# Four transposing DMAs at another place in the tail, and another order of all operations, in a recurrent attention layer with a gated feed-forward

## The chip, the cores and the metric

The kernel runs on one core of one Trainium2 chip. The metric is the device time of one execution in microseconds. Three timed runs of the kernel before gave 998.56, 998.62 and 999.2 us; their median, 998.62 us, is its time.

## The reference

The input is one sequence of 2048 tokens with 640 features, in bf16. It goes through an attention layer with a recurrent memory and then through a gated feed-forward layer, each on the normalised input and each with the residual added.

```python
for s in range(n_seg):                      # 64 segments of 32 tokens
    h = concatenate([mem, xs])              # 8 memory rows, then the 32 tokens
    q, k, v = h @ Wq, h @ Wk, h @ Wv        # 32 heads of 128
    p = softmax(where(mask, q k^T * scale, -1e9))
    o = (p v) @ Wo                          # 40 rows of 640
    mem = o[:8]                             # goes into the next segment
    outs.append(o[8:])
h  = x + attention(layernorm(x))
gate, up = layernorm(h) @ W_gate, layernorm(h) @ W_up    # 640 -> 1728
h2 = h + (gate * (gate > 0) * up) @ W_down
```

The first 8 rows of a segment's output are the memory of the next one, so the 64 segments run one after another. Everything else (the projections of the tokens that are not memory, the feed-forward of finished tokens) can be done at other times.

## The kernel before, in words

**Stages.** The kernel first loads Wq, Wk, Wv and Wo (rows "Wq<-in_A_Wq_dram" and so on) and meanwhile projects part of the tokens ahead (`rest`, for the first nine of sixteen groups of 128 tokens). Then it runs the 64 segments (`segment`). In a segment, TensorE projects Q, K and V (line 1577, five steps for each of six banks, four matmuls of 128x512 per step on strips of 32 columns of the array), forms scores (1954, 1958), sums (1968), the product with V (1993, 1998), and the output projection (2027, 2046, 2063). ScalarE and VectorE evacuate PSUM between them (lines 1411 and 1412 are the two halves of one helper, `copy`), VectorE transposes Q and K (2076). Into the gaps of that chain the kernel puts work that is not urgent: `rest` for later tokens, the output rows of finished token groups (`rest_o`, 1661), and gate and up projections of finished token quarters (`ahead`, 1742), whose results wait in HBM (`scr_g`).

**The tail.** After the last segment the space of the attention weights is free. SyncE loads the feed-forward weights there: W_gate and W_up in three pieces each, in the order columns 512 to 895, 896 to 1663, 0 to 511 (`FPIECES`, loaded by `load_f`, issue line 2164), then W_down and the last 64 columns, and the results that were computed ahead (2177, 2180, 1767). TensorE computes what is left of the gates of the third quarter of tokens (`gates(2)`, matmuls at 1778), the down projections of three quarters (`downs`, 1834), then the gates and down projections of the last quarter (`gates(3)`, `downs(3)`). The last quarter's normalised rows lie in HBM (`scr_n`), and four transposing DMAs, one for each 128 tokens, bring them into `xn2T` with features on partitions (issue line 1771, operation name "xnld"); each can be issued once its rows are written. Line 1834 is the down projection with `again` (1555) as its second half, 1824 that of the last 128 tokens.

**What sets the order.** Nothing in the code is emitted in program order. Every operation is registered with its engine (or a choice of engines), its inputs and outputs, an assumed duration and a name. A list scheduler in the kernel (`_Sched.schedule`) then takes, for each engine in turn, the ready operation of the highest level; the order on each engine's queue, the bank or buffer that an operation gets, and the engine where there is a choice come out of it. An operation's level is the length of the longest chain of assumed durations behind it, plus a bias from a table, and a second bias for the name in one segment:

```python
o.level += self.bias.get(o.name, 0.0) + self.bias.get(f"{o.name}@{o.seg}", 0.0)
```

Segment numbers run from 1 to 64; 0 and below stand for the start, 65 for the tail. `BIAS` holds 3645 such numbers. The weight loads of the tail have biases of their own, 2000 less 20 for each load, set in `load_f`. Evacuations of PSUM are registered through `either`, and `ENGINE`, a table by name and by name and segment, says whether ScalarE ("act") or VectorE ("dve") has them; a name that is not in it goes to whichever the scheduler finds done first. SyncE issues nearly all DMAs, in the order of its queue, one after another.

Of the kernel before, what the change touches and what calls it, by code (L numbers as in the profile page):

```python
# [27 lines left out]
BIAS = {"sel2": -428.53, "ezero": 827.13, "ldxs0": 772.6, "ldxs1": -1075.19, "ldxa": 977.15, "ldxl": -444.97,  # L28
    "ldxx": 94.56, "ldxn": 296.11, "ldxx0": -425.81, "ldxst": -946.28, "ldxxm": -329.88, "ldmev": -440.02,
# [18 lines left out]
    "gx": -75.13, "gxrelu": -736.07, "gxev": -228.23, "gxst": -268.67, "ln2nd": -1166.07, "xnld": 1080.06,  # L48
    "gld": -294.56, "gu": 52.5, "relu": 1032.72, "gmul": -789.51, "roz": -16.73, "tn2go": 142.03,
# [1214 lines left out]
def build_kernel(nc, A_x, A_mem0, A_Wq, A_Wk, A_Wv, A_Wo, A_seg_len, B_x, B_W_gate, B_W_up,  # L1264
# [46 lines left out]
    sel2 = ar.alloc("sel2", [128, 64], BF16)  # L1311
# [21 lines left out]
    oTr = [ar.alloc(f"oTr{i}", [128, H, 32], BF16) for i in range(2)]  # L1333
# [63 lines left out]
    sc = _Sched()  # L1397
# [483 lines left out]
    for nm, b in (("ldxr", 9000.0), ("ldxr1", 8950.0)):  # L1881
        for t in ("", "s0", "s1", "a", "l", "x", "n", "T", "e"):
            sc.bias[nm + t] = b
# [369 lines left out]
```

## Time and profile before

| | us |
|---|---|
| median of the three timed runs | 998.62 |
| the profiled execution, as a whole | 995.62 |
| its span, first to last instruction | 993.9 |
| TensorE busy in it | 973.8 |
| VectorE busy | 618.3 |
| ScalarE busy | 502.4 |
| GpSimd busy | 112.5 |

The profiled execution took 1.72 us more than its span. A row of the timeline is one instruction, or several of one kind that follow each other ("x20"): start, length in us, engine, line, operation, output tile and input tiles, shape, and in brackets the idle time of the engine before it and what ended it. "SPq" is SyncE's queue, where a row is the issue of a DMA and not its transfer. "PEld" is the weight load of TensorE, which runs beside the matmuls; a matmul of 128x512 is recorded with some 379 ns though the next one may start 216 ns after it, so that TensorE can be called busy while it waits a little.

### The profile page before, as it was taken

What the parts mean: (1) busy time and instruction counts of PE and PEld (TensorE: products, weight loads), DVE (VectorE), ACT (ScalarE), POOL (GpSimd) and SP (SyncE); (2) the same over time, 40 slices, a digit from 0 to 9 for tenths busy, and PEclk for the clock granted to TensorE, in tenths of its full rate; (3) what the DMA queues carried; (4) which work ended last, traced back from release to release, by engine and by line L of the source; (5) the groups of instructions that cost most, each with busy time, mean ns of one, the idle gap of its engine ahead of it and who ended that gap; (6) DMA issues with size and microseconds to landing.
All of it is one profiled execution on the core that took longest, in us unless ns stands there. A gap on an engine that the chain in (4) does not pass through costs nothing.

```text
span 993.9 us, 54620 instructions
## 1 busy us (share of the span) xinstructions
PE 973.8 (98%) x25518; PEld 535.7 (54%) x24540; DVE 618.3 (62%) x1345; ACT 502.4 (51%) x1226; POOL 112.5 (11%) x264
## 2 busy tenths in 40 slices
PE   7989999999999999999999999999999999999998
PEld 4334565555555555655555556555555565543343
DVE  5835767768676766576666676767656766523232
ACT  2236555556565565555555565555555656521020
POOL 2341011111011011001000010000100000100000
PEclk9999999999999999999999999999999999999999
DMA  8996122223131323232232234333223352289211
GB/s 320 403 350 145 45 57 57 66 53 92 36 89 39 85 76 83 55 81 66 67 84 62 78 105 86 86 93 79 52 72 89 76 102 76 68 260 288 72 41 40
DMA packets 181553, 103.62 MB, mean 104 GB/s; under 512 B 126212, under 2 KB 177484, under 8 KB 181324
## 3 DMA queue, kind: packets, MB, share of 16 engines
q1 hardware_dynamic: 175948, 95.51, 34.5%
q10 hardware_dynamic: 5376, 4.63, 1.4%
q8 instruction: 196, 3.21, 1.3%
q14 instruction: 33, 0.27, 0.1%
HBM read 67.30 MB, written 29.75 MB: 98 GB/s over the span
## 4 chain that ended last, share of the span: by engine, by line
PE 90%; DMA 4%; SPq 3%; DVE 1%; issue 1%; ACT 0%; POOL 0%; ACTq 0%; DVEq 0%; POOLq 0%
PE ps L1577 49%; PE ps L2046 7%; PE ps L1742 7%; PE ps L2027 7%; PE ps L1834 4%; PE ps L1661 3%; PE ps L1778 3%; PE ps L1993 3%; DMA scr_qk<-stg 3%; PE ps L1555 2%; PE ps L1968 2%; PE ps L1954 1%; SPq L2164 1%; DMA Wq<-in_A_Wq_dram 1%; DMA scr_o<-osr 1%
## 5 line engine op out<-in xcount | busy, mean ns | idle before, releaser
L1411 ACT ACTIVATE tok<-ps 128x512 bf16<-128x512 f32 x216 | 128.2, 597 | 146.5 <-PE ps L1577 141.4
L1577 PE MATMUL ps<-Wk,xT 128*32 128x512 bf16 x2560 | 180.4, 379 | 0.4 <-ACT tok L1411 0.4
L1577 PE MATMUL ps<-Wv,xT 128*32 128x512 bf16 x2560 | 176.3, 379 | 0.0
L1577 PE MATMUL ps<-Wq,xT 128*32 128x512 bf16 x2560 | 170.1, 379 | 0.5 <-DVE tok L1412 0.3
L2076 DVE STREAM_TRANSPOSE QT<-tok 128x512 bf16<-128x512 bf16 x128 | 90.6, 708 | 47.5 <-ACT tok L1411 45.4
L1577 PEld LDWEIGHTS ps<-Wq,xT 128*32 128x32 bf16 x2560 | 70.6, 97 | 66.5 <-DVE xT L1691 9.1
L2076 DVE STREAM_TRANSPOSE KT<-tok 128x512 bf16<-128x512 bf16 x128 | 90.8, 709 | 24.6 <-ACT tok L1411 22.7
L1577 PEld LDWEIGHTS ps<-Wk,xT 128*32 128x32 bf16 x2560 | 68.4, 96 | 55.6 <-DVE xT L1691 2.9
L1963 ACT ACTIVATE E<-ps 128x224 bf16<-128x224 f32 x128 | 45.7, 357 | 81.4 <-PE ps L1958 77.7
L2046 PE MATMUL ps<-Wo,oT 128*32 128x160 bf16 x4096 | 83.5, 233 | 1.0 <-issue 1.0
L2046 PEld LDWEIGHTS ps<-Wo,oT 128*32 128x32 bf16 x4096 | 74.1, 97 | 15.5 <-ACT oT L1411 5.6
L2027 PE MATMUL ps<-Wo,oT 128*32 128x320 bf16 x2048 | 81.5, 300 | 0.9 <-DVE oT L1412 0.8
L1577 PEld LDWEIGHTS ps<-Wv,xT 128*32 128x32 bf16 x2560 | 61.0, 96 | 38.8 <-ACT tok L1411 0.7
L1412 DVE CAST oT<-ps 128x320 bf16<-128x320 f32 x124 | 55.0, 485 | 42.9 <-PE ps L1998 36.9
L1940 POOL COPY QT<-RS 128x256 bf16<-128x256 bf16 x64 | 25.7, 402 | 470.4 <-PE ps L1958 470.2
L1411 ACT ACTIVATE Vm<-ps 128x512 bf16<-128x512 f32 x122 | 72.0, 591 | 11.4 <-PE ps L1577 6.3
L1412 DVE CAST tok<-ps 128x512 bf16<-128x512 f32 x104 | 68.7, 661 | 9.6 <-PE ps L1577 9.3
L2027 PEld LDWEIGHTS ps<-Wo,oT 128*32 128x32 bf16 x2048 | 52.7, 96 | 27.3 <-DVE oT L1412 7.7
L1688 DVE CAST_PREDICATED xm<-turn,ps 128x64 bf16<-128x64 uint16 x126 | 27.9, 222 | 61.3 <-PE ps L1555 61.1
L2011 POOL COPY oTr<-oT 128x128 bf16<-128x128 bf16 x128 | 41.0, 320 | 193.5 <-ACT oT L1411 110.4
L1411 ACT ACTIVATE oT<-ps 128x320 bf16<-128x320 f32 x132 | 50.4, 436 | 11.5 <-PE ps L1998 11.1
L1411 ACT ACTIVATE ps<-seed 128x384 f32<-128x384 bf16 x117 | 54.4, 489 | 2.1 <-DVE half L2035 1.8
(108 smaller groups left out, 1453.5 us busy)
## 6 DMA issues: line engine op xcount, KB each, us to landing
RS<-scr_qk SPq DMA_DIRECT2D x63, 128.0 KB, 2.3
big<-in_A_x_dram SPq DMA_DIRECT2D x34, 160.0 KB, 2.8
Wq<-in_A_Wq_dram SPq DMA_DIRECT2D x10, 512.0 KB, 7.7
Wk<-in_A_Wk_dram SPq DMA_DIRECT2D x10, 512.0 KB, 8.2
Wv<-in_A_Wv_dram SPq DMA_DIRECT2D x10, 512.0 KB, 8.6
Wo<-in_A_Wo_dram SPq DMA_DIRECT2D x8, 640.0 KB, 11.2
Wgs<-in_B_W_gate_dram SPq DMA_DIRECT2D x30, 160.0 KB, 3.0
Wus<-in_B_W_up_dram SPq DMA_DIRECT2D x30, 160.0 KB, 2.9
```

The source lines that it names most:

```text
L1411: return e.activation(dst, src, ACTF.Copy)
L1412: return e.tensor_copy(dst, src)
L1577: o = pe.matmul(out, lhs[c], rhs, start=(c == 0), stop=(c == DC - 1), skip_group_check=True)
L1661: o = pe.matmul(bank(bk)[p0:p0 + 32, 0:2 * SLICE], oTr[b][:, h, :], cols(h, 2 * a, 2 * a + 2), start=(h < 2), stop=(h >= H - 2), skip_grou ...
L1742: o = pe.matmul(bank(bk)[32 * i:32 * i + 32, 0:512], wt[:, c, 32 * i:32 * i + 32], xn2T[0][:, :, c * 128:(c + 1) * 128], start=(c == 0), s ...
L1778: o = pe.matmul(bank(bk)[:, 0:TB], lhs(c), xT[:, :, c * 128:(c + 1) * 128], start=(c == 0), stop=(c == DC - 1))
L1834: pe.matmul(bank(ba)[:, 0:512], lhs, Wd[:, j, 0:512], start=(j == 0), stop=(j == FC - 1), skip_group_check=True)
L1963: op("act", lambda a: a.activation(E[:, g, :, 0:56], sco(BS[g]), ACTF.Exp, scale=SCALE), r=["table"], w=[("E", g)], x=[BS[g]], dur=0.36, n ...
L2011: op("pool", lambda e: e.tensor_copy(oTr[ob][:, 16 * g:16 * g + 16, XR * y:XR * y + XR], oT[:, 16 * g:16 * g + 16, 0:XR]), r=[("oT", g, 0) ...
L2027: o = pe.matmul(bank(BA)[p0:p0 + 32, 0:2 * SLICE], oT[:, h, XR:40], cols(h, 2 * b2, 2 * b2 + 2), start=(i == 0 and jj < 2), stop=(i == 3 a ...
L2046: o = pe.matmul(bank(BW)[32 * j:32 * j + 32, 0:SLICE], oT[:, 16 + 4 * jj + i, XR:40], cols(h, j, j + 1), start=(i == 0 and jj == 0), stop= ...
L2076: op("dve", lambda v, tb=tb, dst=dst: v.transpose(dst, tok[tb.at][:, :].rearrange("p (h r) -> p h r", r=32)), w=[("QT" if p == 0 else "KT" ...
```

## The change

The scheduler, the operations and their assumed durations stay. The two tables are replaced: nearly every number of `BIAS` differs (3728 numbers now, from 3645; median difference of a number of one segment some 30), and `ENGINE` has 476 entries in place of 453, many for other names and segments. In the tail, the bias of "xnld" at 65 goes from 60.36 to -200.0, which together with its general bias (1080.06, now 1082.02) lowers the level of the four transposing DMAs by some 258, beneath that of the loads up to the up weights' second piece. Q0ev, V0ev, rvev, ldmev and ldxr1e, evacuations that had a fixed engine as a rule, have one now only where an entry for the segment says so. The operations that normalise the first tokens (names "ldxr" and "ldxr1" with their endings), which had fixed biases of 9000 and 8950, take theirs from the table. As entries by segment stand for the 64 segments, V0ev was fixed on ScalarE in 64 and is now in 21 (free in 43); Q0ev was in 61 and is now in 31 (on VectorE in 4, free in 29).

```diff
-    "tn2nd@65": 46.22, "hld@65": -14.3, "outdma@65": 0.74, "xnld@65": 60.36}
...
-    "ervev": "act", "r0ev": "dve", "r0Tev": "act", "r1ev": "act", "rvev": "dve", "Q0ev": "act", "Q0Tev": "act",
-    "K0ev": "act", "K0Tev": "act", "V0ev": "act", "Q1ev": "dve", "Q1Tev": "dve", "K1ev": "act", "K1Tev": "act",
...
+    "outdma@65": -14.29, "xnld@65": -200.0}
+ENGINE = {"ldxre": "dve", "er0ev": "dve", "er0Tev": "act", "er1ev": "act", "ervev": "act", "r0ev": "dve",
+    "r0Tev": "act", "r1ev": "act", "Q0Tev": "act", "K0ev": "act", "K0Tev": "act", "Q1ev": "dve", "Q1Tev": "dve",
+    "K1ev": "act", "K1Tev": "act", "seed0": "act", "seed1": "act", "oTev0": "dve", "oTev1": "act",
...
     for nm, b in (("ldxr", 9000.0), ("ldxr1", 8950.0)):
         for t in ("", "s0", "s1", "a", "l", "x", "n", "T", "e"):
-            sc.bias[nm + t] = b
+            sc.bias[nm + t] = BIAS.get(nm + t, b)
```

More of the change, by code (lines that the diff above doesn't have):

```diff
@@ L27 @@
 FPIECES = ((512, 896), (896, 1664), (0, 512))
-BIAS = {"sel2": -428.53, "ezero": 827.13, "ldxs0": 772.6, "ldxs1": -1075.19, "ldxa": 977.15, "ldxl": -444.97,
-    "ldxx": 94.56, "ldxn": 296.11, "ldxx0": -425.81, "ldxst": -946.28, "ldxxm": -329.88, "ldmev": -440.02,
[18 rows of a table removed]
-    "gx": -75.13, "gxrelu": -736.07, "gxev": -228.23, "gxst": -268.67, "ln2nd": -1166.07, "xnld": 1080.06,
-    "gld": -294.56, "gu": 52.5, "relu": 1032.72, "gmul": -789.51, "roz": -16.73, "tn2go": 142.03,
[632 rows of a table removed]
-ENGINE = {"ldxre": "act", "ldxr1e": "act", "ldmev": "act", "er0ev": "dve", "er0Tev": "act", "er1ev": "act",
-    "ervev": "act", "r0ev": "dve", "r0Tev": "act", "r1ev": "act", "rvev": "dve", "Q0ev": "act", "Q0Tev": "act",
-    "K0ev": "act", "K0Tev": "act", "V0ev": "act", "Q1ev": "dve", "Q1Tev": "dve", "K1ev": "act", "K1Tev": "act",
-    "seed0": "act", "seed1": "act", "oTev0": "dve", "oTev1": "act", "osrev": "act", "ldxre@0": "act",
[81 rows of a table removed]
+BIAS = {"sel2": -402.81, "ezero": 831.38, "ldxrs0": 9027.86, "ldxrs1": 8963.02, "ldxra": 9858.42,
+    "ldxrl": 9196.87, "ldxrx": 9327.74, "ldxrn": 8693.49, "ldxrT": 8853.69, "ldxre": 8894.01, "ldxs0": 1066.65,
+    "ldxs1": -1150.79, "ldxa": 1103.68, "ldxl": -408.5, "ldxx": 58.04, "ldxn": 450.6, "ldxx0": -414.49,
[20 rows of a table added]
+    "gx": -75.13, "gxrelu": -784.38, "gxev": -233.43, "gxst": -413.2, "ln2nd": -1187.92, "xnld": 1082.02,
+    "gld": -187.88, "gu": -5.39, "relu": 1098.67, "gmul": -624.07, "roz": -58.15, "tn2go": 358.47,
[650 rows of a table added]
+ENGINE = {"ldxre": "dve", "er0ev": "dve", "er0Tev": "act", "er1ev": "act", "ervev": "act", "r0ev": "dve",
+    "r0Tev": "act", "r1ev": "act", "Q0Tev": "act", "K0ev": "act", "K0Tev": "act", "Q1ev": "dve", "Q1Tev": "dve",
+    "K1ev": "act", "K1Tev": "act", "seed0": "act", "seed1": "act", "oTev0": "dve", "oTev1": "act",
+    "osbev": "act", "osrev": "act", "ldxre@0": "dve", "ldxr1e@0": "dve", "ldmev@0": "act", "er0ev@-1": "dve",
[87 rows of a table added]
 class _Slot:
```

1486 rows, old and new, of tables (BIAS, ENGINE) are left out of this document.

## The prediction

> **What bounds the kernel now.** I read the page first, then the busy time by stretches, then the tail as a timeline of SyncE and TensorE. The page:
>
> ```profile
> span 993.9 us, 54620 instructions
> PE 973.8 (98%) x25518; PEld 535.7 (54%) x24540; DVE 618.3 (62%) x1345; ACT 502.4 (51%) x1226; POOL 112.5 (11%) x264
> PE 90%; DMA 4%; SPq 3%; DVE 1%; issue 1%; ACT 0%; POOL 0%; ACTq 0%; DVEq 0%; POOLq 0%
> ```
>
> TensorE is called busy for 973.8 of 993.9 us and carries 90% of the chain that ended last, so a new order can win only time in which TensorE stands still. The stretches say where (columns: stretch, length, then busy time with the count for TensorE, its weight loads, VectorE, ScalarE, GpSimd, then granted clock, DMA share, GB/s):
>
> ```profile
> 0.00:60.00 60.00, 52.07 (x1028) 25.25 (x1032) 41.11 (x76) 18.99 (x42) 22.90 (x50) 1.00 0.98 364
> 60.00:80.00 20.00, 16.94 (x284) 7.00 (x276) 3.79 (x10) 8.27 (x19) 3.50 (x4) 0.91 1.07 299
> 80.00:100.00 20.00, 18.34 (x572) 10.37 (x556) 11.76 (x25) 12.65 (x31) 4.19 (x8) 1.00 0.50 124
> 100.00:865.00 765.00, 762.62 (x22576) 440.82 (x21833) 519.91 (x1159) 440.92 (x1092) 79.09 (x197) 1.00 0.29 72
> 865.00:884.50 19.50, 17.92 (x346) 8.86 (x323) 7.09 (x13) 8.40 (x19) 2.78 (x6) 1.00 0.66 196
> 884.50:994.00 109.50, 105.97 (x742) 43.39 (x530) 34.61 (x65) 13.20 (x25) 0.00 (x0) 1.00 0.42 131
> ```
>
> Idle is length less busy: 7.93, 3.06 and 1.66 us in the first three, 12.65 us in all; 2.38 us in the 765 us of the segments; 1.58 and 3.53 us in the two tail stretches. In the first 60 us the DMA engines are filled (0.98), and order gains little there. At 60 to 80 us the granted clock is 0.91, which costs another 0.09 x 20 = 1.8 us.
>
> The 2.38 us of the middle is too small, because matmul ends are modelled: a record of 379 ns covers a wait behind it. So I count its work at the pace at which groups follow each other when nothing holds them. Counts: first the projections (L1577), second the gate and up groups run ahead (L1742), each alone in that stretch, then the output projections (L2046, L2027, L1661):
>
> ```profile
> 100.00:865.00 765.00, 495.74 (x8224) 209.85 (x8228) 1.00 0.29 72
> 100.00:865.00 765.00, 87.52 (x1240) 29.11 (x1240) 1.00 0.29 72
> ```
>
> ```profile
> L2046 PE MATMUL ps<-Wo,oT 128*32 128x160 bf16 x3912 | 79.8, 233 | 0.7 <-issue 0.6
> L2027 PE MATMUL ps<-Wo,oT 128*32 128x320 bf16 x1952 | 77.7, 300 | 0.0
> L1661 PE MATMUL ps<-Wo,oTr 128*32 128x320 bf16 x896 | 41.0, 299 | 0.0
> ```
>
> Pace, from the start of one merged row to the start of the next:
>
> ```profile
> 414.70 0.27 PE L1954 MATMUL ps<-QT,KT 128*32 128x40 bf16 x16
> ...
> 414.83 0.60 PE L1577 MATMUL ps<-Wv,xT 128*32 128x512 bf16 x8
> 415.37 0.27 PE L1993 MATMUL ps<-E,Vm 32*128 32x40 bf16 x16
> ...
> 415.71 0.39 PE L1577 MATMUL ps<-Wv,xT 128*32 128x512 bf16 x4
> ...
> 416.30 1.27 PE L2027 MATMUL ps<-Wo,oT 128*32 128x320 bf16 x32
> 417.50 0.27 PE L1993 MATMUL ps<-E,Vm 32*128 32x40 bf16 x16
> ...
> 418.45 0.44 PE L1661 MATMUL ps<-Wo,oTr 128*32 128x320 bf16 x8
> 418.72 1.28 PE L2046 MATMUL ps<-Wo,oT 128*32 128x160 bf16 x64
> 419.83 0.24 PE L2063 MATMUL ps<-half,sel 128*32 128x160 bf16 x4
> ...
> 419.97 0.39 PE L1742 MATMUL ps<-xn2T,Wus 128*32 128x512 bf16 x4
> ...
> 420.89 1.25 PE L1577 MATMUL ps<-Wq,xT 128*32 128x512 bf16 x20
> 421.97 1.25 PE L1577 MATMUL ps<-Wk,xT 128*32 128x512 bf16 x20
> ```
>
> Twenty matmuls of 512 columns take 421.97 - 420.89 = 1.08 us, so 8224 + 1240 of them take 9464 / 20 x 1.08 = 511 us. L2046: 3912 / 64 x 1.11 = 68 us; L2027: 1952 / 32 x 1.20 = 73 us; L1661: 896 / 8 x 0.27 = 30 us. A half segment's scores take 0.13 us and its value product with the sums 0.34 us, the final add 0.14 us: 1.08 us in each of some 61 segments, 66 us. Together 748 us of 765: about **17 us of stalls** in the middle, 0.28 us a segment, spread thin. What order can reach at all is 17 + 12.65 + 1.8 = 31 us plus the tail's waits.
>
> **Part 1, the transposing DMAs.** The tail of SyncE (start, length; these are issues) and of TensorE:
>
> ```profile
> 874.65 0.37 SPq L2164 DMA_DIRECT2D Wg<-in_B_W_gate_dram  x1
> 875.06 2.94 SPq L1771 DMA_TRANSPOSE xn2T<-scr_n  x2
> 878.04 0.58 SPq L2164 DMA_DIRECT2D Wu<-in_B_W_up_dram  x1
> ```
>
> ```profile
> 880.70 2.32 PE L1778 MATMUL ps<-xn2T,Wg 128*128 128x512 bf16 x10
> 884.22 1.25 PE L1778 MATMUL ps<-xn2T,Wu 128*128 128x512 bf16 x5 [1.21 <-DMA Wu<-in_B_W_up_dram]
> ```
>
> Two of the four transposes stand between the second gate piece and the second up piece and hold SyncE for 2.94 us; TensorE then waits for that up piece, by the record 1.21 us. Ten matmuls take 2 x 1.08 us, so the true loss is 884.22 - 880.70 - 2.16 = 1.36 us. Behind the up piece, the transposes cost nothing new if it lands by 880.70 + 2.16 = 882.86. Its bytes need this pipe:
>
> ```profile
> 877.00:878.00 1.00, 1.00 (x6) 0.49 (x5) 0.34 (x1) 0.17 (x1) 0.00 (x0) 1.00 1.05 398
> 878.00:879.00 1.00, 1.00 (x7) 0.42 (x5) 0.34 (x1) 0.20 (x1) 0.00 (x0) 1.00 1.05 385
> 879.00:880.00 1.00, 1.00 (x6) 0.46 (x5) 0.18 (x1) 0.39 (x1) 0.00 (x0) 1.00 1.25 230
> ```
>
> Each piece is 640 x 768 x 2 bytes = 0.98 MB. From about 876.5 us two of them at 385 GB/s take 5.1 us, to 881.6; with a few tenths for the landing that is 882, in time. The slice of 879 us, where the transposes run, moves only 230 GB/s. I take the whole **1.3 us**; bounds 0 (the pipe is the limit) and 1.4. The transposes' cover: the last token quarter's gates need all four, and the fourth was issued last:
>
> ```profile
> 925.83 1.21 SPq L1771 DMA_TRANSPOSE xn2T<-scr_n  x1
> ```
>
> so the two moved ones may be issued anywhere up to there and hide behind down projections; without that cover, each costs its issue, 1.5 us. Queued behind the moved issues on SyncE are the third gate and up pieces and the down weights, if the transposes land directly behind the up piece: these shift earlier by the up piece's place and no later than now.
>
> [...]
>
> **Part 2, the order.** Every bias of the list scheduler is new, and where evacuations may run: V0's had ScalarE in all 64 segments and now in 21, free in 43; Q0's in 61, now in 31, with 29 free and 4 on VectorE. No instruction, transfer or byte is added or removed. Nothing in the trace prices an order that has not run, so I bound it: for the gain, a quarter of the 31 us above, 7.7 us; for the loss, 6 us (second rival). I take a gain of **2.3 us**, a thirteenth of the pool: the stalls are spread over some 120 short waits, which a reordering partly trades against each other, and the first 60 us are held by transfers.
>
> **The sum.** The profiled execution took 995.62 us (span 993.9 plus 1.72 around it): 995.62 - 1.3 - 2.3 = 992.0. The three timed runs have a median of 998.62, 3.0 above the profiled one; the same offset gives **995.0 us**, 0.36% faster.
>
> **Rivals.** (a) Only the transposes count, and the order breaks even: 998.62 - 1.3 = 997.3, no change that can be told (0.2% is 2.0 us, about what a measurement of this kernel can tell). For it: waits that are short everywhere. Against it: 1.66 and 3.06 us in one place each before 100 us.
>
> (b) Slower. VectorE gets evacuations that ScalarE had, and the transposes of K come behind them:
>
> ```profile
> L2076 DVE STREAM_TRANSPOSE KT<-tok 128x512 bf16<-128x512 bf16 x123 | 87.2, 709 | 24.0 <-ACT tok L1411 22.0
> L1412 DVE CAST tok<-ps 128x512 bf16<-128x512 f32 x83 | 54.9, 661 | 3.9 <-PE ps L1577 3.7
> ```
>
> ```profile
> PEld ps L1954 <- DVE KT L2076: 19.3, 81, 0.3
> ```
>
> The scores' weight load already waits for that transpose 81 times in the middle, 0.24 us each, under a running matmul (379 ns recorded, 216 ns to the next: 0.16 us of cover). One evacuation of 0.661 us ahead of it costs 0.50 us. If half of the 72 freed evacuations of V0 and Q0 go to VectorE and a third of those stand before a transpose, that is 12 x 0.50 = 6 us: 998.62 - 1.3 + 6 = 1003.3. It decides from about 7 such places on, where it eats the gains of both parts and makes 1.3 + 2.3 = 3.6 us.
>
> (c) A larger gain: the stretch of 60 to 100 us closes its idle 4.7 us by half and keeps its clock (1.8 us), and the middle gives 3: 998.62 - 1.3 - 2.4 - 1.8 - 3 = 990.1. For it: the clock dip is a single event. Against: DMA share 1.07 at 60 to 80. [...]
>
> (d) The move does nothing: the up piece is limited by the pipe, or the transposes fall elsewhere ahead of a piece. Then only the order's 2.3 us: 996.3.
>
> **How the numbers follow.** Forecast 995.0: 0.30 (own range 993 to 996.5); (d) 0.08; (c) 0.15; (a) 0.19; (b) 0.28. Faster by over 0.2% are the forecast, (c) and (d): 0.53. Within 0.2%: (a), 0.19. Slower: (b), 0.28. Both signs hold weight, so the range runs from near (c) to (b): 989 to 1003, with a tenth beyond each end.
>
> **What would show it.** Right: the second up piece issued at most 0.6 us after the second gate piece, no wait for it on TensorE near 883 us, transposes of the last quarter behind it; 100 to 865 us shorter by 1 to 3 us; 60 to 80 us at a clock over 0.91 for (c). Wrong: a longer stretch of segments with more waits on VectorE's K transposes (b), a wait on a gate or up piece elsewhere in the tail (d), or idle that moved from one stretch to the next.

## The result, and the profile after

After: median of 20 timed runs 1001.33 us (997.71 to 1003.80). Before, run beside it on the same chip: 999.03 us (996.65 to 1000.87, 20 runs). The ratio is **1.0023, 95% interval [1.0013, 1.0033]**: the change makes the kernel slower by 2.3 us, where 3.6 us less were predicted. The profiled execution of after took 1001.09 us. That of before, 995.62 us, lies below all of the 20 timed runs of before, so the two profiles differ by more than the two kernels do. The page of after:

```profile
span 999.3 us, 54612 instructions
PE 973.2 (97%) x25509; PEld 538.0 (54%) x24540; DVE 607.8 (61%) x1319; ACT 512.1 (51%) x1252; POOL 112.2 (11%) x264
PE 87%; DMA 3%; SPq 2%; ACTq 1%; issue 1%; DVE 1%; ACT 1%; POOL 0%; DVEq 0%; POOLq 0%
```

TensorE is busy as long as before, and the span is longer: idle time was added. The stretches of after, with the columns of the prediction:

```profile
60.00:80.00 20.00, 16.15 (x292) 7.03 (x280) 3.71 (x10) 8.28 (x20) 3.16 (x3) 1.00 0.86 260
100.00:865.00 765.00, 761.38 (x22576) 441.74 (x21832) 507.61 (x1128) 450.68 (x1117) 79.09 (x198) 1.00 0.29 72
865.00:884.50 19.50, 19.50 (x393) 9.91 (x374) 9.31 (x18) 8.14 (x19) 2.77 (x6) 1.00 0.54 170
884.50:999.30 114.80, 106.96 (x738) 43.75 (x535) 34.53 (x65) 14.38 (x27) 0.00 (x0) 1.00 0.44 131
```

The stretch around 883 us has lost its idle time (1.58 us before), the last one has 7.84 us (3.53 before). The tail of SyncE after (issues):

```profile
877.15 0.37 SPq L2191 DMA_DIRECT2D Wg<-in_B_W_gate_dram  x1
877.56 1.06 SPq L2191 DMA_DIRECT2D Wu<-in_B_W_up_dram  x1
878.66 0.53 SPq L2191 DMA_DIRECT2D Wg<-in_B_W_gate_dram  x1
879.23 2.87 SPq L1798 DMA_TRANSPOSE xn2T<-scr_n  x1
882.15 0.59 SPq L2191 DMA_DIRECT2D Wu<-in_B_W_up_dram  x1
882.78 5.46 SPq L2191 DMA_DIRECT2D Wd<-in_B_W_down_dram  x2
888.29 2.18 SPq L1798 DMA_TRANSPOSE xn2T<-scr_n  x1
...
898.11 0.43 SPq L1794 DMA_DIRECT2D gT<-scr_g  x1
898.58 0.54 SPq L2141 DMA_DIRECT2D scr_o<-osb  x1
...
906.91 1.30 SPq L1702 DMA_DIRECT2D scr_o<-osr  x2
...
930.08 1.21 SPq L1798 DMA_TRANSPOSE xn2T<-scr_n  x1
```

The second up piece now follows its gate piece after 0.41 us. But the two transposes don't stand directly behind it. One stands between the third gate and up pieces and one behind the down weights, and they hold SyncE for 2.87 + 2.18 = 5.05 us, where the two together took 2.94 us before. The last segment's output write (scr_o<-osb), right behind the second up piece before, stands behind gT now: 21.9 us after the first gate matmul, where it was issued 4.5 us after it before. TensorE's tail after:

```profile
876.71 2.33 PE L1805 MATMUL ps<-xn2T,Wg 128*128 128x512 bf16 x10
...
883.20 2.32 PE L1805 MATMUL ps<-xn2T,Wg 128*128 128x512 bf16 x10
885.36 1.24 PE L1805 MATMUL ps<-xn2T,Wu 128*128 128x512 bf16 x5
...
898.79 1.25 PE L1805 MATMUL ps<-xn2T,Wl 128*128 128x512 bf16 x5 [1.17 <-DMA Wl<-in_B_W_up_dram]
...
903.30 0.22 PE L1582 MATMUL ps<-Wd,gT 128*128 128x128 bf16 x1 [0.71 <-ACT osf L1438]
...
914.51 0.39 PE L1861 MATMUL ps<-Wd,gT 128*128 128x512 bf16 x1 [1.75 <-DVE osr L1697]
...
932.92 1.25 PE L1805 MATMUL ps<-xn2T,Wl 128*128 128x512 bf16 x5 [1.12 <-DMA xn2T<-scr_n]
```

From the first gate matmul to the end of the span, which I call the **tail**, after takes 999.3 - 876.7 = 122.6 us and before 993.9 - 874.2 = 119.7. The 1.21 us wait for the up piece is gone, and 1.17 + 0.71 + 1.75 + 1.12 = 4.75 us of other waits stand in its place. Before has only one more than the up piece's:

```profile
PE ps L1778 <- DMA Wu<-in_B_W_up_dram: 1.2, 1, 1.2
PE ps L1834 <- DVE osr L1670: 0.4, 1, 0.4
```

### The profile page after: what moved, and what is told of

Its sections match the earlier page's. It is cut to its first block, busy times and chain, and to the rows that moved or that the text cites. A ratio compares the mean times of both kernels' runs of the same rounds, so it can differ in the third digit from the quotient of the medians.

```text
span 999.3 us, 54612 instructions
## 1 busy us (share of the span) xinstructions
PE 973.2 (97%) x25509; PEld 538.0 (54%) x24540; DVE 607.8 (61%) x1319; ACT 512.1 (51%) x1252; POOL 112.2 (11%) x264
## 4 chain that ended last, share of the span: by engine, by line
PE 87%; DMA 3%; SPq 2%; ACTq 1%; issue 1%; DVE 1%; ACT 1%; POOL 0%; DVEq 0%; POOLq 0%
PE ps L1604 46%; PE ps L2073 7%; PE ps L2054 7%; PE ps L1769 7%; PE ps L1805 5%; PE ps L1688 3%; PE ps L2020 3%; PE ps L1861 2%; PE ps L1995 2%; PE ps L1582 2%; PE ps L1981 1%; DMA scr_n<-big 1%; DMA scr_v<-stg 1%; DMA scr_o<-osr 1%; ACTq L1648 1%
## 5 line engine op out<-in xcount | busy, mean ns | idle before, releaser
L1438 ACT ACTIVATE tok<-ps 128x512 bf16<-128x512 f32 x227 | 134.5, 597 | 141.4 <-PE ps L1604 122.3
L2073 PEld LDWEIGHTS ps<-Wo,oT 128*32 128x32 bf16 x4096 | 74.1, 97 | 17.4 <-ACT oT L1438 6.5
L1967 POOL COPY QT<-RS 128x256 bf16<-128x256 bf16 x64 | 25.6, 401 | 444.4 <-PE ps L1985 444.1
L1439 DVE CAST tok<-ps 128x512 bf16<-128x512 f32 x93 | 61.5, 661 | 13.0 <-PE ps L1604 12.8
L2062 DVE TENSOR_TENSOR half<-ps,half 128x320 bf16<-128x320 f32 x64 | 31.4, 491 | 38.0 <-ACT half L1438 37.5
```

Source lines behind the costliest of these rows:

```text
L1438: return e.activation(dst, src, ACTF.Copy)
L1439: return e.tensor_copy(dst, src)
L2062: op("dve", lambda v: v.tensor_tensor(half[1][:, :], bank(BA)[:, 0:2 * SLICE], half[0][:, :], ALU.subtract), r=["half0"], w=["half1"], x=[ ...
L2073: o = pe.matmul(bank(BW)[32 * j:32 * j + 32, 0:SLICE], oT[:, 16 + 4 * jj + i, XR:40], cols(h, j, j + 1), start=(i == 0 and jj == 0), stop= ...
```

## The experiments

All twelve kernels compute everything. Each is before or after with one to three numbers of the table changed, in e9 and e11 also with one operation under a name of its own, in e12 with two. Each ratio is against before, run beside it on the same chip; e1 to e4, e5 to e8, e9 and e10, and e11 and e12 ran on four chips, where before had medians of 1000.55, 998.98, 999.28 and 999.71 us. The tail is that of each kernel's own profiled execution, rounded after the subtraction. "The named part" is the one number that moves the four transposes.

| kernel | median us | ratio, 95% interval | tail us |
|---|---|---|---|
| after | 1001.33 | 1.0023 [1.0013, 1.0033] | 122.6 |
| e1 before, transposes at -200 | 1001.79 | 1.0015 [1.0000, 1.0030] | 121.8 |
| e2 after, transposes back at 60.36 | 998.82 | 0.9984 [0.9969, 0.9998] | 119.8 |
| e3 before, transposes at 40 | 999.26 | 0.9993 [0.9980, 1.0006] | 119.5 |
| e4 after, transposes at 40 | 997.48 | 0.9976 [0.9961, 0.9991] | 119.6 |
| e5 after, last output write early | 1000.17 | 1.0014 [1.0001, 1.0027] | 121.1 |
| e6 after, last columns early | 1001.98 | 1.0024 [1.0010, 1.0038] | 121.5 |
| e7 e4 with last columns early | 998.61 | 0.9991 [0.9978, 1.0005] | 118.8 |
| e8 e3 with last columns early | 999.49 | 1.0004 [0.9993, 1.0015] | 119.8 |
| e9 e4, gT ahead of three h loads | 998.69 | 0.9994 [0.9981, 1.0006] | 120.8 |
| e10 e4 once more | 998.22 | 0.9994 [0.9980, 1.0009] | 119.4 |
| e11 after, late gate on last columns | 1003.44 | 1.0036 [1.0022, 1.0050] | 125.8 |
| e12 e9, late gate on last columns | 1000.63 | 1.0009 [0.9997, 1.0021] | 120.8 |

**Which half of the change costs the time.** e1 puts only the number of the named part into before, e2 takes only that number back out of after.

```diff
-"xnld@65": 60.36
+"xnld@65": -200.0
```

> The kernel before with the four transposes' tail bias at -200.0 alone; the segments keep their order. Theory T (the tail pays): in the changed kernel's trace the tail, from its first gate matmul to the end, is 122.6 us against 119.7, with new waits of 1.2, 0.7, 1.8 and 1.1 us; this kernel has the same tail queue, so it is 2.5 to 3.5 us slower than before. Rival S (the segments pay): the tail is only unlucky in that one execution and the move frees the 1.3 us of the up piece, so this kernel is 1 us faster or the same.

```diff
-"xnld@65": -200.0
+"xnld@65": 60.36
```

> The changed kernel with the tail bias of the four transposes put back to 60.36; the segments keep the new order, SyncE's tail queue is that of before. Theory T: tail of 119.7 us again and a time within 1 us of before (the new order as such is worth -1 to +1). Rival S: 2 to 3.5 us slower than before, because the first gate matmul still comes 2.5 us later.

The named part alone makes before slower (1.0015, at the edge of what can be told). Without it after is faster than before (0.9984), and the intervals of after and e2 don't touch: 0.0039, or 3.9 us, lie between them. The tails say the same: 119.7 and 119.8 us without the move, 121.8 and 122.6 with it. The waits of e1's tail, where the order is that of before:

```profile
PE ps L1835 <- DVE osr L1671: 1.5, 1, 1.5
PE ps L1779 <- DMA Wl<-in_B_W_up_dram: 1.1, 1, 1.1
PE ps L1556 <- ACT osf L1412: 0.7, 1, 0.7
PE ps L1779 <- DMA xn2T<-scr_n: 0.4, 1, 0.4
```

They are the four of after. So the loss lies in the named part. Whether the new order of the segments is a gain by itself is less sure: e2's interval ends at 0.9998, and e1 and after, the same pair of orders with the move in both, don't show it.

**The exchange as it was read.** At 40 the two transposes fall right behind the second up piece and nothing else changes place. e3 is before with that exchange alone (the order of every other engine is that of before), e4 is after with it.

```diff
-"xnld@65": 60.36
+"xnld@65": 40.0
```

> The kernel before with the tail bias at 40.0: only the two transposes and the second up piece change places on SyncE's queue, every other instruction of every engine stays where it was. Both theories: no wait for the up piece near 883 us, 1.2 to 1.4 us faster than before. If the transfers are the limit instead, the wait stays and the time is the same within 0.3 us.

```diff
-"xnld@65": -200.0
+"xnld@65": 40.0
```

> The changed kernel with the tail bias at 40.0: new order of the segments, and the exchange of two places alone. Theory T: 1.3 us less than the kernel with the bias put back to 60.36, so 0.3 to 2.3 us faster than before. Rival S: 1 to 2 us slower than before.

This is the move that the prediction priced at 1.3 us. Its tail is 119.5 against 119.7 us in the old order, 119.6 against 119.8 in the new one: 0.1 to 0.2 us. The ratios, 0.9993 against 1 and 0.9976 against 0.9984, differ by 0.0007 and 0.0008, each less than its interval. e3's TensorE shows where the 1.3 us went:

```profile
878.09 2.33 PE L1779 MATMUL ps<-xn2T,Wg 128*128 128x512 bf16 x10
...
884.58 2.32 PE L1779 MATMUL ps<-xn2T,Wg 128*128 128x512 bf16 x10
886.74 1.24 PE L1779 MATMUL ps<-xn2T,Wu 128*128 128x512 bf16 x5
...
900.44 1.24 PE L1779 MATMUL ps<-xn2T,Wl 128*128 128x512 bf16 x5 [0.35 <-DMA Wl<-in_B_W_up_dram]
...
903.52 0.22 PE L1556 MATMUL ps<-Wd,gT 128*128 128x128 bf16 x1 [0.37 <-issue]
```

The up piece is not waited for (886.74 - 884.58 = 2.16 us, the pace of ten matmuls). But the first down projection starts 903.52 - 878.09 = 25.43 us after the first gate matmul, only 0.5 us earlier than before (900.13 - 874.21 = 25.92). It needs gT, the gates that were computed ahead. The rows of the DMA views (last column: us from issue to landing), first of before, then of e3:

```profile
gT<-scr_g SPq DMA_DIRECT2D x1, 512.0 KB, 6.6
```

```profile
gT<-scr_g SPq DMA_DIRECT2D x1, 512.0 KB, 5.6
```

In before gT was issued at 893.16 and landed at 899.8, 0.3 us ahead of its first use; in e3 issued at 897.63 (the timeline of SyncE), landed at 903.2, again 0.3 us ahead. The loads that stand ahead of gT on SyncE are the same in both. So the wait for the up piece hid behind the landing of gT: TensorE came early to the next load. A 0.8 us wait for osr, 0.4 in before, took most of the rest. e2 shows the same from the other side: it waits 1.8 us for the up piece, and its tail of 119.8 us is only 0.1 us longer than e4's, which doesn't.

**Two places that might carry the loss.** e5 is after with the last segment's output write ahead of the second gate piece; e6 is after with the loads of the last 64 columns ahead of the down weights. e7 and e8 put e6's places into e4 and e3.

```diff
+BIAS.update({"odma@64": 1975.85})
```

> The changed kernel with the last segment's output write put ahead of the second gate piece (its bias for segment 64 raised by 2000); the transposes stay at -200.0. Theory W (the late write is what the tail pays: the chain to the last transposed rows starts from it): the wait of 1.1 us for the transposed rows near 932 us goes, the tail comes from 122.6 to 121 us or less, about 1 to 2 us faster than the changed kernel. Rival Q (SyncE's queue as a whole is later): the waits of 1.2 us for the last weight columns and of 1.8 us for the output rows stay and the tail stays within 0.5 us of 122.6.

```diff
+BIAS.update({"ldf48@65": 60.0, "ldf49@65": 60.0})
```

> The changed kernel with the loads of the last 64 weight columns ahead of the down weights; the transposes stay at -200.0. If each wait of the tail stands for itself, the 1.2 us for these columns go and the rest stay: tail of 121.4 us, 1.2 us faster than the changed kernel. If the end of the next wait is set by SyncE's queue, the wait for the output rows grows by what was gained: tail still near 122.5 us.

```diff
+BIAS.update({"xnld@65": 40.0, "ldf48@65": 60.0, "ldf49@65": 60.0})
```

> New order of the segments, the transposes directly behind the second up piece (40.0), and the last 64 weight columns ahead of the down weights. If the 0.9 us wait for those columns was what swallowed the up piece's gain, the tail falls from 119.6 to 118.5 us or less, and the time is 0.3 to 0.4% below before. If the next wait takes it, it stays at 119.6 and 0.24% below.

> The same two places with the order of the kernel before in the segments. Against the kernel with both places and the new order it shows what that order is worth with a clean tail: 1.5 us more if the pairs so far (0.9984 and 0.9976 against 1 and 0.9993) hold, the same if they were noise.

Neither place alone carries it. In e5 the wait for the last transpose is gone, but the tail is still 121.1 us. Its two longest waits, the first of them at the first down projection:

```profile
PE ps L1583 <- issue: 2.1, 1, 2.1
PE ps L1862 <- DVE osr L1698: 0.6, 1, 0.6
```

The longer one is again a wait for gT, issued at 898.47 and landed 5.3 us later, 0.3 us ahead of the matmul at 904.04. e5 also gives the cleanest comparison with e2: in the two traces ScalarE, VectorE and GpSimd run the same operations in the same order, TensorE does so in the tail, and only SyncE's queue differs. Its transposes stand as in after, and the output write stands early. The tail is 1.4 us longer than e2's (121.13 against 119.77), and the ratios, 1.0014 and 0.9984, have intervals that don't touch. So SyncE's order with the transposes moved costs time though no other engine's order changes.

In e6 the waits for the last columns and the last transpose are gone, and two others have come, of 2.2 us for the rows of h and 1.5 us for osf:

```profile
PE ps L1862 <- DVE tl L1869: 2.2, 1, 2.2
PE ps L1583 <- ACT osf L1439: 1.5, 1, 1.5
```

The first of the two is the wait for osr in another place: the addition into tl that TensorE waited for stood behind the second addition into osr, for which VectorE had waited 11.00 us.

In e7 and e8 the loads of the last columns are no longer waited for, and one wait at the first down projection has come in their place, 1.1 us in e7 and 2.0 in e8. The profile puts it down to osf. But in e8 osf was done at 902.97 us, the first down projection came at 904.50, and gT, issued at 894.36 with 9.8 us to land, was there at 904.16: the wait is for gT, here as at 903.30 in after. The tails, 118.8 and 119.8 us, lie around those of e4 and e3, and the ratios can't be told from 1.

**Is gT the bound?** e9 is e4 with the load of gT under a name of its own, and raised past three loads of h rows. e10 is e4 again.

```diff
-           chan=("wb", 8), name="gld", xfer=done * 0.33, desc=40)
+           chan=("wb", 8), name="gldq", xfer=done * 0.33, desc=40)
...
+BIAS.update({"gldq": 900.0, "xnld@65": 40.0})
```

> Before's pure exchange with the new order of segments (as in the run with one place and the new order), and the load of the gates computed ahead (gT, 512 KB) issued ahead of three of the four loads of h rows that stood before it (3 x 164 KB) instead of behind them. Theory L (the first down projection waits for the landing of gT, which is set by the bytes queued ahead of it): gT lands 3 x 164 KB / 385 GB/s = 1.3 us earlier against the first gate matmul, at about 24.3 us after it, the first down projection starts about 24.7 us after it instead of 25.5 to 26.0, and the tail is 0.9 to 1.3 us shorter than that of the run beside it, unless a later load (the h rows, gTs) is then late. Rival N (the end of the tail is set by a later load or by the evacuations): the first down projection starts earlier, but the tail stays at 119.5 +- 0.4 us, with as much idle time on the h rows, gTs or osr as was won. Rival P (gT was not the bound): the first down projection starts at 25.5 or later although gT lands earlier.

> The new order of segments with the pure exchange once more, for comparison in the same call. If the gain of the order is real, the ratio is again 0.9965 to 0.9990 against before; if the former result (0.9976) was chance, it lies at 0.999 to 1.001. First down projection 25.5 to 26.0 us after the first gate matmul, 0.3 to 0.4 us after the landing of gT, tail 119.5 +- 0.4 us.

In e9 gT was issued at 894.66, 15.99 us after the first gate matmul at 878.67. The DMA view has 8.3 us to its landing, so it landed 24.3 us after that matmul, as expected, but the first down projection came at 25.5:

```profile
901.55 1.24 PE L1806 MATMUL ps<-xn2T,Wl 128*128 128x512 bf16 x5 [0.89 <-DMA Wl<-in_B_W_up_dram]
902.72 1.54 PE L1689 MATMUL ps<-Wo,oTr 128*32 128x320 bf16 x40
904.19 0.39 PE L1862 MATMUL ps<-Wd,gT 128*128 128x512 bf16 x1
...
933.07 1.25 PE L1806 MATMUL ps<-xn2T,Wl 128*128 128x512 bf16 x5 [1.32 <-DMA xn2T<-scr_n]
```

So theory L fell in this form: gT isn't the only bound. With the last columns early (e7, e8) gT sets the start of the down projections, and with gT early the load of the last columns, waited for 0.89 us, sets nearly the same start. The tail even grew to 120.8 us. The scheduler, seeing gT early, rearranged TensorE's tail, and a wait of 1.32 us for the last transpose appeared: the very wait of after.

e10 brings the ratio of e4 from 0.9976 to 0.9994; the two intervals overlap, and the mean is 0.9985.

**What after, e1, e6 and e9 have in common.** In the order that the scheduler wrote for TensorE, the first gate of the last quarter, which needs all four transposes, stands behind 98 down projections on gTs in before, e2 to e5, e7, e8 and e10, and behind 84 in after, e1, e6 and e9. In before the last transposing DMA is issued at 925.83 and takes 2.8 us to land, so it is there at 928.6; in after at 930.08 + 2.8 = 932.9:

```profile
xn2T<-scr_n SPq DMA_TRANSPOSE x1, 2.8
```

```profile
929.20 1.24 PE L1778 MATMUL ps<-xn2T,Wl 128*128 128x512 bf16 x5
```

Those are the landing (the DMA view of before; after's has the same row) and the gate in before's timeline; after's gate started at 932.92. So the gate started 54.99 us into the tail before and 56.21 after: 1.22 us later, with 14 down projections more still to do behind it. Down projections run in pairs, one of 512 columns and one of 128, which follow each other every 0.27 us (914.79, 915.06, 915.33 in after's timeline), so 14 are 1.9 us. From this gate to the end of the span after needs 999.3 - 932.9 = 66.4 us and before 993.9 - 929.2 = 64.7. That is 1.7 us more, and 1.2 + 1.7 = 2.9 us is the tail's whole loss. This divides the loss; it does not show yet that the 14 projections cause it.

The waits say more. The tail less the sum of TensorE's waits in it is 119.7 - 1.6 = 118.1 us in before, 122.6 - 4.75 = 117.9 in after, 121.8 - 3.7 = 118.1 in e1, 121.1 - 3.5 = 117.6 in e5, and between 117.5 and 118.1 us in every kernel here but e11. So work that stands behind that gate instead of ahead of it is not lost by that, and the waits are the loss. The 14 projections could at most have filled the wait for the last transpose, 1.12 us in after and 0.36 in e1. The rest arises earlier: after is 0.7 us behind before at the first down projection (26.59 us into the tail against 25.92), 1.8 at the matmul that waits for osr (37.80 against 35.96), and 2.9 at the end.

The 0.7 us are gT's. Into the tail, it was issued at 18.95 us in before, 19.54 in e3, 20.40 in e4, 21.36 in e1, 21.40 in after and 22.14 in e5, and landed at 25.6, 25.1, 25.6, 26.3, 26.3 and 27.4: some lateness of the issue costs nothing, and what comes after about 21 us does.

e11 and e12 put more down projections ahead of that gate. The gate on the last columns in the last quarter gets a name of its own and a lower number, in after and in e9.

```diff
-            op("pe", f, r=[key] + list(more) + xk, w=list(writes), x=[bk] + list(hold), dur=1.08, n=10, mode="f", name="gu")
+            op("pe", f, r=[key] + list(more) + xk, w=list(writes), x=[bk] + list(hold), dur=1.08, n=10, mode="f", name="guL" if b == 3 and key == "Wl" else "gu")
...
+BIAS.update({"guL": -100.0})
```

> After, with one change on TensorE's queue alone: the last quarter's gate on the last 64 columns (Wl) stands behind 126 down projections of gTs instead of behind 84 (before and the faster runs have 98, after, the named part alone and the gates load early have 84, and these are the ones that waited for the last transposing DMA). Theory D (TensorE was given too little to do ahead of the landing of the last transposing DMA): 42 matmuls more, 21 pairs of 0.27 us or 5.7 us, stand ahead of the first gate that needs it, more than the 1.1 us that TensorE waited; that wait goes, and the tail is 1.1 us shorter than after's 122.6, about 121.5, 0.0010 less than after's ratio of 1.0023. Rival S (the time goes into another wait): the wait for osr or for the gate on the last columns at the end takes it, and the tail stays at 122.3 or above.

> The run with the gates load early, with the same change on TensorE's queue (126 down projections of gTs ahead of the last quarter's gate on the last 64 columns instead of 84). Theory D: its wait of 1.3 us for the last transposing DMA goes, and the tail falls from 120.8 to about 119.5. Rival S: the tail stays at 120.5 or above, with the wait elsewhere.

The wait for the last transpose went in both, and the tails did not get shorter: rival S held. The gate moved further than intended, to near the end of the queue, where the last down projections need its result. The longest wait of e12's tail:

```profile
PE ps L1853 <- DVE gT L1831: 1.4, 1, 1.4
```

1.3 us were exchanged for 1.4. So these two runs don't decide whether the 14 projections alone would bring back the wait for the last transpose. A kernel with SyncE's order of after and TensorE's tail of before was not tried without other changes; e5 is the nearest to it (up to the last load of gTs its SyncE differs from after's by the place of the output write alone) and has 121.1 us. The remaining 1.5 us of after lie in that place and in what was rearranged with it; these runs don't part the two.

**Why the last transpose is late.** VectorE in after and in before, at the second addition into osr (the output rows of the last token groups, half by half through one buffer):

```profile
913.97 0.48 DVE L1697 TENSOR_TENSOR osr<-ps,osf 64x320 bf16<-64x320 f32 x1 [2.39 <-DMA scr_o<-osr]
```

```profile
909.63 0.48 DVE L1670 TENSOR_TENSOR osr<-ps,osf 64x320 bf16<-64x320 f32 x1 [0.68 <-DMA scr_o<-osr]
```

The addition waits until the first half has been written out. That write stands on SyncE behind all that the tail loads: it was issued 903.37 - 874.21 = 29.2 us into the tail before and 906.91 - 876.71 = 30.2 after. The addition came at 35.4 and 37.3 us, TensorE's 1.75 us wait for osr is a wait for it, and the second write, the normalisation and the last transpose (landed at 54.4 and 56.2 us) follow from it. Of the 1.8 us by which the addition is later, 1.0 is the later issue; the other 0.8 us passed between issue and addition (6.3 us before, 7.1 after), and why is not shown. VectorE's queue was rearranged too: this addition stands behind two additions into tl before, and behind one in after and e1, and VectorE stands still for it longer (2.39 against 0.68 us). So the one late stretch of SyncE appears in TensorE's waits for gT, for osr and for the last transpose.

## Why the prediction was wrong

**Part 1 failed, and with it the sign.** The wait for the up piece went as predicted: issue 0.41 us behind the gate piece, no wait near 885 us. Three sentences around it did not hold.

- "I take the whole 1.3 us". The exchange as it was priced is worth 0.1 to 0.2 us of the tail (e3, e4). I asked whether the up piece could land in time and not which load was late next, though gT lands 0.3 us before its use in the trace of before. The bound of 0 was right, though its reason was not the pipe ahead of the up piece but the load behind it. The few tenths for the landing were an estimate: in after the up piece, issued at 877.56 us, took 7.3 us to land (the DMA view), so it was there at 884.9, 8.2 us into the tail, where 882 stood for 7.8 and 882.86 for 8.65.
- "Behind the up piece, the transposes cost nothing new if it lands by 880.70 + 2.16 = 882.86" and "so the two moved ones may be issued anywhere up to there and hide behind down projections". Their results do hide. Their issues don't: they hold SyncE for 5.05 us in place of 2.94, in a stretch where gT and what stands behind it are waited for within a few tenths of a us. By e5 against e2, SyncE's order alone costs 1.4 us of the tail. How much of that is the 2.1 us of longer issues was not measured by itself: at 40, too, the transposes hold SyncE longer than before (3.39 us in e3, 3.68 in e4), and there the tail doesn't suffer.
- "these shift earlier by the up piece's place and no later than now". The condition, that they land directly behind the up piece, was false. The number -200 put one behind the third gate piece and one behind the down weights. It also moved the last output write 17.4 us later in the tail, and gave TensorE and VectorE another order there. The move costs 1.5 us by the times of e1 and before, 3.9 by those of after and e2, 2.1 and 2.8 by the tails of the same pairs.

**Part 2 can't be told from nothing.** 2.3 us were taken. Where tails are alike, the new order gives 0.0016 (e2 against before) and 0.0008 (the mean of e4 and e10 against e3): 0.8 to 1.6 us. e7 against e8 gives 0.0013, but there the tail is 1.0 us shorter, which leaves 0.3. After against e1 goes the other way by 0.0008, about as much as its tail is longer (0.8 us). e2's interval ends close to 1, at 0.9998, and e4's low ratio did not come again in e10. The traces show no gain: from the final add of the first segment to that of the last, the four executions with the old order took 787.2 to 789.8 us, 788.4 in the mean, and the ten with the new order 786.2 to 790.2, 788.1 in the mean. So the sum as measured is +2.9 us from the tail and, by what is left of the +2.3, some -0.6 from all else, which is less than the scatter.

**The rivals.** (d) came nearest in mechanism: the transposes did fall elsewhere ahead of a piece. Its price of nothing was the error. (a), that the order breaks even, fits what can be told of the order, but it counted the transposes as a gain. (b), slower by VectorE, had the sign by a mechanism that didn't happen. VectorE took fewer of the evacuations, 93 where the grouped view of before has 104, and its K transposes are waited for as before (19.3 us, 81 times):

```profile
L1439 DVE CAST tok<-ps 128x512 bf16<-128x512 f32 x93 | 61.5, 661 | 13.0 <-PE ps L1604 12.8
```

```profile
PEld ps L1981 <- DVE KT L2103: 18.6, 80, 0.3
```

(c) can't be read from one execution. After kept full clock at 60 to 80 us and yet had 3.85 us idle there. e4 and e10, the same kernel on two chips, reached the first gate matmul at 874.30 and 876.35 us. Between 60 and 80 us the clock dipped in e4 and not in e10, whose dip came in the first 60 us (0.97 there):

```profile
60.00:80.00 20.00, 17.36 (x288) 7.44 (x272) 3.37 (x10) 8.25 (x20) 2.94 (x3) 0.91 0.86 262
```

```profile
60.00:80.00 20.00, 16.17 (x296) 7.25 (x288) 3.80 (x10) 7.44 (x19) 3.81 (x4) 1.00 0.87 265
```

Two microseconds between two executions is as much as either part was to bring, so the head can only be judged by many timed runs, while the tails of the two agree within 0.3 us. The profiled times of before and after, 5.5 us apart where the medians are 2.3 apart, have 2.9 us from the tails; the rest shows that.

## What to carry to other kernels

When a wait on a load is taken away, look up the landing of every later load on the same queue against its first use: the gain is what the tightest of them leaves (in e3 and e4 0.1 to 0.2 us of the 1.3). A number in a list scheduler's table names a rank and not a place, so read the emitted order of every queue, the stores and the other engines too, before pricing a move. Judge a part of a kernel by its own length from one instruction to another, and let many timed runs decide what lies below the scatter of one execution.

## What the runs showed of the hardware

**The same issue took 1.21 to 2.87 us in after.** The same kind of transposing DMA held SyncE for 2.87 and 2.18 us in the stretch of after where the weights are loaded (372 GB/s from 879 to 882 us, 358 from 888 to 890), for 1.23 us at 923 us (26 GB/s from 923.1 to 924.3), and for 1.21 us at 930 us, when nothing else was moving (0 GB/s from 930 to 931). The rate alone does not tell the length: in before one took 1.97 us at 921 us and one 1.21 us at 926 us, both with 72 GB/s moving (920.8 to 922.8 us, 925.8 to 927.0). What holds an issue was not measured by itself.

**Half clock behind a wait of 2.77 us.** TensorE in e11 (timeline, then the granted clock in slices of 1 us):

```profile
915.14 0.39 PE L1862 MATMUL ps<-Wd,gT 128*128 128x512 bf16 x1 [2.77 <-DVE osr L1698]
```

```profile
916.00:917.00 1.00, 1.00 (x7) 0.27 (x3) 0.20 (x1) 0.00 (x0) 0.00 (x0) 0.61 0.87 304
917.00:918.00 1.00, 1.00 (x5) 0.30 (x2) 0.03 (x1) 0.00 (x0) 0.00 (x0) 0.50 0.31 103
918.00:919.00 1.00, 1.00 (x6) 0.30 (x2) 0.97 (x3) 0.00 (x0) 0.00 (x0) 0.50 0.74 268
919.00:920.00 1.00, 1.00 (x7) 0.25 (x2) 0.59 (x2) 0.30 (x2) 0.00 (x0) 0.69 0.52 170
```

From about 916.2 us, some 1 us behind the wait, the clock was half for 3.4 us, which is 0.39 + 0.50 + 0.50 + 0.31 = 1.7 us lost: a pair of down projections took 0.53 us there (916.78, 917.31, 917.84 in e11's timeline) and 0.27 us ahead of it (915.42, 915.69, 915.97). That, the wait's 1.0 us over after's, and 1.4 us for the late gate, less the 1.1 us that went, make 3.0 of the 3.2 us by which e11's tail exceeds after's. It is also why e11 alone falls out of the reckoning above: its tail less its waits (6.0 us) is 119.8 us, and less the 1.7 us 118.1.

The length of one wait does not tell whether a drop follows. The waits of 2.1 and 2.2 us in e5 and e6 were followed by none (a clock of 1.00 in every stretch from 875 to 980 us), but before, which has the 0.91 between 60 and 80 us, ran at half clock from 71.0 to 74.4 us (0.50 in three slices of 1 us, then 0.79), 0.9 us behind a wait of only 1.55 us that ended at 70.07. Nor does the idle time seen in the 3.4 us ahead of a drop, as long as the drop itself, tell it: it was 1.9 us in before and 2.3 in e11, and e5 and e6, with 2.1 and 2.2 us in one wait, kept full clock. What sets off a drop is not shown.
